# A starting stage by token halves, and one-hot rows of later pairs in an earlier step, in a kernel of clustered attention and two mixers

## The chip, the cores and the metric

The kernel runs on one core of one Trainium2 chip. The metric is device microseconds of one execution, launch included; the time before is the median of three runs.

## The reference, cut to what matters

Three layers in a row, with a float32 result; U, V and the weights arrive as 64-bit floats. The first is attention with 2 batches, 8 heads, 768 tokens and 64 numbers per head, where a query sees only the keys of its own cluster:

```python
q_assign = np.argmax(np.einsum('bhsd,hcd->bhsc', q_n, c_n), axis=-1)   # 16 clusters a head
k_assign = np.argmax(np.einsum('bhsd,hcd->bhsc', k_n, c_n), axis=-1)
mask = q_assign[:, :, :, None] == k_assign[:, :, None, :]
scores = np.where(mask, scale * np.matmul(q, k.transpose(0, 1, 3, 2)), -1000000000.0)
attn = np.exp(scores - np.max(scores, axis=-1, keepdims=True))
out = np.matmul(attn / (np.sum(attn, axis=-1, keepdims=True) + 1e-09), v)
```

Behind it stand a mixer over tokens of rank 32 (`U`, `V`) with a feed-forward part of 2048 channels, and a gated convolution mixer of 1024 channels. The change touches the attention's beginning and its helpers alone.

## The kernel before, in words

All five engines are programmed by hand: instructions of each engine run in the order in which the code emits them, and tiles carry the waits between engines. Heads go in pairs (8 pairs of 2 heads), a head in 6 tiles of 128 queries, so there are 96 steps of attention; step `n` is tile `n` in the order of heads, and `s = n % 12` is its place in its pair.

Float32 products are made of float32r matmuls of high and low parts. For one head, `ab` (128 rows) and `cd` (80 rows) are the score operands: `ab` holds parts of q and k and what is left of them after rounding, `cd` the rounded parts in rows 0 to 63 and the one-hot clusters of the query and key in rows 64 to 79, the key's scaled by 2 to the 60th, so that a pair of different clusters gets a huge negative score. For head 0 of pair 0, ScalarE and GpSimd make them from the raw tiles `rq` and `rk` (L187 to L193). For all other heads three DMAs from the POOL queue load them (`load_ops`, L104) and GpSimd subtracts (`split_ops`, L120). `load_raw` (L89) brings `rq` and `rk` of a pair on the SP queue, `load_v` (L111) the values.

Clusters of a pair: `sims` (L198) multiplies raw q and k with the normed centroids on TensorE, `sims_onehot` (L209) makes a one-hot in five VectorE operations (part 0 to 4), `onehot_t` (L228) turns it on TensorE into `oht`, `onehot_rows` (L235) copies it to `os` on ScalarE and sends its rows into `cd` with four DMAs on the SP queue. For the first pair, head 0's rows are copied directly, by ScalarE (L239) and VectorE (L240). Before the loop stand matmuls on zeros, `warm(count)` (L150), whose result nobody reads.

One `step(n)` (L577) emits, in this order: scores of tile n+2 (`s_mm`, of which `s_mm_ab` is the first half), a third of the product with the values of group g (`pv_mm`; a group is three tiles), `fin_t` of the group before (which makes `at`) or a piece of the token mixing, `sims` of the next pair when s is 2, six transposes of tile n (`t_mm`), then on ScalarE and VectorE the split of the transposed tile n-1 (`t_hi`, `t_lo`), the exponential of tile n+1 (`s_exp`), the row maximum of tile n+2 (`s_max`), the finish of a group (`fin_a` into `asb`, `fin_x`), and `prep(n)`. `fin_x` (L347) copies a finished group into `ats` on ScalarE, GpSimd then adds its halves and multiplies three tiles into `x`. `ats` has one buffer. `prep(n)` (L543) emits the work for the next pair by a table of places: one-hot parts at s = 2, 2, 3, 4, 5, raw loads and head 0's loads at 0, its split at 2, the values at 3, head 1's loads at 4, its split at 5, one-hot transposes and rows at 7.

Weights are turned from 64-bit words to float32 in jobs by `pump` (L410): in the attention loop every second step advances the one job on its way by one place of the plan `THIN` (L407): load, `job_base` on ScalarE, `job_low`, `job_high`, `job_sign` on VectorE, and put (ScalarE and GpSimd). Seven jobs belong to the loop: U, two halves of V, and four pieces of the first feed-forward chunk.

Score tiles have two PSUM buffers, so scores of tile n+2 wait for the exponential of tile n. Transposes, `at`, `oht` and similarities share three PSUM buffers (`ps_t`).

Of the kernel before, what the change touches and what calls it, by code (L numbers as in the profile page):

```python
# [24 lines left out]
P = 128  # L25
# [6 lines left out]
def tile_kernel(ctx: ExitStack, tc: tile.TileContext, qk, vv, cen, u_w, v_w, w1, w2, win, wout, conv, out):  # L32
# [55 lines left out]

    def load_raw(b, p):  # L89
        rq = a_raw.tile([P, S], F32, tag="rq", name="rq")  # L90
        rk = a_raw.tile([P, S], F32, tag="rk", name="rk")
        h0 = 2 * p
        nc.sync.dma_start(out=rq, in_=qk[b, h0:h0 + 2, :, 0, :].rearrange("h d s -> (h d) s"))
        nc.sync.dma_start(out=rk[D:2 * D], in_=qk[b, h0, :, 1, :])
        nc.sync.dma_start(out=rk[0:D], in_=qk[b, h0 + 1, :, 1, :])
        raw[b, p] = (rq, rk)

# [29 lines left out]

    cent = acon.tile([P, 2, D], F32, name="cent")
# [47 lines left out]
    nc.tensor.transpose(pc, cent.rearrange("p a d -> p (a d)"), identf)  # L176
    warm(4)
# [20 lines left out]
    def sims(b, p):  # L198
        rq, rk = raw[b, p]
        pm = ps_t.tile([P, NT * 4, NC], F32, tag="t", name="sim")  # L200
        for t in range(NT):
# [32 lines left out]

    def onehot_rows(b, p, first=False):  # L235
        pt = ohst.pop((b, p))["pt"]
        if first:
            cd = ops[b, 2 * p][1]
            nc.scalar.activation(cd[D:D + NC, 1], pt[2 * NC:3 * NC], AF.Copy, scale=BIG, bias=-BIG)  # L239
            nc.vector.tensor_copy(cd[D:D + NC, 0], pt[0:NC])  # L240
# [302 lines left out]
    def prep(n):  # L543
# [331 lines left out]
```

## Time and profile before

| | |
|---|---|
| median of three runs (lowest, highest) | 686.99 us (686.22, 689.02) |
| the profiled execution | 687.29 us |
| its span | 685.5 us |
| TensorE busy | 669.8 us (98%) |
| VectorE, ScalarE, GpSimd busy | 445.1, 373.1, 301.5 us |
| mean granted TensorE clock | 0.992 |

The span goes from the first to the last instruction; 1.8 us of the execution lie around it. A busy TensorE is not one at its peak, since matmuls overlap and their ends are modelled; how far apart the starts of equal matmuls lie says more. Times in rows are microseconds from the start of the span.

### The profile page before, as it was taken

To read this page: it belongs to the slowest core of one execution; us is meant where nothing else is said; L and a number is where in the kernel's file an instruction comes from. 1 tells how busy PE (TensorE), PEld (TensorE's weight loads), DVE (VectorE), ACT (ScalarE), POOL (GpSimd) and SP (SyncE) were. 2 spreads that over 40 slices of the span, in tenths; PEclk is the share of its full clock that TensorE was granted. 3 is DMA by queue.
4 is the path that set the end of the run, shared out by engine and by line. 5 is a ranking of instruction groups with operands and counts; after the bars stand their busy time and mean duration, and the time that the engine had idled before them with its cause. 6 is when DMAs were issued, how large, how long until landed. Compare 5 with 4: busy or idle time off the path is not lost.

```text
span 685.5 us, 10463 instructions
## 1 busy us (share of the span) xinstructions
PE 669.8 (98%) x3782; PEld 587.7 (86%) x3782; DVE 445.1 (65%) x825; ACT 373.1 (54%) x744; POOL 301.5 (44%) x391
## 2 busy tenths in 40 slices
PE   8899999999999999999999999999999999999997
PEld 6789989899999998888888888888887788888886
DVE  3888888887988898658732878775247545643400
ACT  3787869787877898425311343432133357753611
POOL 6667656676757533425530333332024644322300
PEclk8899999999999999999999999999999999999999
DMA  8986867775756611212210443342014000000111
GB/s 188 131 178 132 194 111 179 126 180 93 181 99 145 120 47 32 93 32 93 93 32 3 133 137 124 127 145 71 1 46 133 7 0 1 1 32 15 44 49 47
DMA packets 31827, 61.58 MB, mean 90 GB/s; under 512 B 15808, under 2 KB 19008, under 8 KB 31776
## 3 DMA queue, kind: packets, MB, share of 16 engines
q1 hardware_dynamic: 15632, 40.08, 19.6%
q0 software_dynamic: 16144, 20.84, 17.2%
q8 instruction: 30, 0.49, 0.3%
q14 instruction: 21, 0.17, 0.1%
HBM read 56.29 MB, written 3.15 MB: 87 GB/s over the span
## 4 chain that ended last, share of the span: by engine, by line
PE 79%; DVE 9%; issue 4%; POOL 3%; ACT 3%; DMA 2%; ACTq 0%; SPq 0%; POOLq 0%; DVEq 0%
PE g L764 10%; PE pv L328 7%; PE tr L304 6%; PE h L641 6%; PE h L642 6%; PE h L643 6%; PE a L657 5%; PE a L658 5%; PE a L659 5%; PE sc L266 4%; PE sc L277 3%; PE po L799 3%; PE po L798 3%; PE po L800 3%; PE sim L203 2%
## 5 line engine op out<-in xcount | busy, mean ns | idle before, releaser
L442 POOL TENSOR_TENSOR wl<-wx,wh 128x512 fp32r<-128x512 f32 x48 | 63.3, 1321 | 113.1 <-ACT wh L441 112.8
L317 DVE TENSOR_TENSOR pl<-tr,ph 128x384 fp32r<-128x384 f32 x192 | 97.5, 548 | 20.4 <-ACT ph L313 19.9
L313 ACT CAST ph<-tr 128x384 fp32r<-128x384 f32 x192 | 83.8, 487 | 23.5 <-PE tr L304 23.1
L283 DVE TENSOR_SCALAR_CACHE_REDUCE e<-sc 128x768 f32<-128x768 f32 x96 | 90.7, 945 | 1.9 <-PE sc L277 1.9
L646 ACT ACTIVATE rh<-h 128x512 fp32r<-128x512 f32 (+1 forms) x52 | 29.3, 563 | 112.0 <-PE h L643 112.0
L295 ACT ACTIVATE e<-sc,nb 128x768 f32<-128x768 f32 x96 | 88.1, 918 | 3.9 <-DVE e L283 3.7
L304 PE MATMUL tr<-identf,e 128*128 128x128 f32 x576 | 84.5, 278 | 4.3 <-DVE pl L317 2.5
L647 DVE SCALAR_TENSOR_TENSOR rl<-h,rh 128x512 fp32r<-128x512 f32 (+1 forms) x52 | 33.6, 647 | 83.2 <-ACT rh L646 83.2
L641 PE MATMUL h<-uh,wh 128*128 128x512 f32 (+1 forms) x208 | 78.1, 375 | 1.4 <-DVE rl L647 1.4
L657 PE MATMUL a<-rh,wh 128*128 128x512 f32 (+1 forms) x208 | 78.1, 376 | 0.5 <-DVE xa L673 0.5
L304 PEld LDWEIGHTS tr<-identf,e 128*128 128x128 f32 x576 | 66.8, 142 | 13.3 <-DVE pl L317 8.4
L658 PE MATMUL a<-rl,wh 128*128 128x512 f32 (+1 forms) x208 | 77.7, 373 | 0.3 <-DVE rl L647 0.3
L659 PE MATMUL a<-rh,wl 128*128 128x512 f32 (+1 forms) x208 | 77.6, 373 | 0.0
L643 PE MATMUL h<-uh,wl 128*128 128x512 f32 (+1 forms) x208 | 77.6, 373 | 0.0
L642 PE MATMUL h<-ul,wh 128*128 128x512 f32 (+1 forms) x208 | 77.6, 373 | 0.0
L328 PE MATMUL pv<-ph,vt 128*128 128x384 f32 x192 | 65.6, 342 | 0.2 <-ACT asb L337 0.2
L328 PE MATMUL pv<-pl,vt 128*128 128x384 f32 x192 | 64.9, 338 | 0.0
L266 PE MATMUL sc<-ab 128*128 128x384 f32 x192 | 58.6, 388 | 2.8 <-ACT e L295 2.1
L441 ACT CAST wh<-wx 128x512 fp32r<-128x512 f32 x48 | 29.8, 620 | 57.5 <-DVE wx L395 57.3
L781 POOL TENSOR_TENSOR h<-h,cv 128x768 f32<-128x768 f32 x16 | 29.6, 1851 | 64.5 <-ACT cv L780 64.5
L391 DVE SCALAR_TENSOR_TENSOR wx<-wb,wx 128x512 int32<-128x512 int32 (+3 forms) x52 | 48.8, 938 | 11.3 <-ACT wb L382 9.3
L277 PE MATMUL sc<-cd 80*128 80x384 f32 x192 | 49.8, 341 | 0.5 <-DVE cd L240 0.5
(129 smaller groups left out, 1500.0 us busy)
## 6 DMA issues: line engine op xcount, KB each, us to landing
raw<-in_w_dram SPq DMA_DIRECT2D x32, 512.0 KB, 3.8
ab<-in_qk_dram POOLq DMA_DIRECT2D x30, 384.0 KB, 5.4
cd<-in_qk_dram POOLq DMA_DIRECT2D x15, 384.0 KB, 6.6
raw<-in_win_dram SPq DMA_DIRECT2D x8, 512.0 KB, 3.6
raw<-in_wout_dram SPq DMA_DIRECT2D x8, 512.0 KB, 3.7
rq<-in_qk_dram SPq DMA_DIRECT2D x8, 384.0 KB, 4.1
rk<-in_qk_dram SPq DMA_DIRECT2D x16, 192.0 KB, 4.5
rv<-in_vv_dram SPq DMA_DIRECT2D x8, 384.0 KB, 5.7
```

The source lines that it names most:

```text
L266: nc.tensor.matmul(ps[:, f, 0:HS], ab[:, 0, c0:c0 + P], ab[:, 1, f * HS:(f + 1) * HS], start=True, stop=False)
L283: nc.vector.tensor_scalar(out=e, in0=ps[:, :, 0:HS], scalar1=-SCALE, scalar2=3e38, op0=ALU.mult, op1=ALU.min, accum_out=nb,)
L295: nc.scalar.activation(e, ps[:, :, 0:HS], AF.Exp, scale=SCALE, bias=nb, accum_out=st["sum", n // 3][:, n % 3:n % 3 + 1])
L304: nc.tensor.transpose(pt[:, k, :], e[:, i, k * P:(k + 1) * P], identf)
L317: nc.vector.tensor_sub(lo, st.pop(("t", n, i)), hi)
L328: nc.tensor.matmul(acc, vt[:, h % 2, k, :], m[:, k].rearrange("p a b -> p (a b)"), start=(k == 0 and i == 0), stop=(k == NT - 1 and i == 1),)
L641: nc.tensor.matmul(ph, wh[:, k, ws], uh[g][:, k, ts], start=(k == 0), stop=False)
L642: nc.tensor.matmul(ph, wh[:, k, ws], ul[g][:, k, ts], start=False, stop=False)
L643: nc.tensor.matmul(ph, wl[:, k, ws], uh[g][:, k, ts], start=False, stop=(k == ND - 1))
L657: nc.tensor.matmul(accs[d][:, 0:n], wh[:, i, ds_], rh, start=(f == 0), stop=False)
L658: nc.tensor.matmul(accs[d][:, 0:n], wh[:, i, ds_], rl, start=False, stop=False)
L659: nc.tensor.matmul(accs[d][:, 0:n], wl[:, i, ds_], rh, start=False, stop=(f == NH - 1))
```

## The change

The first pair's q and k are loaded and cast by halves of 384 tokens, in the order in which they are used. VectorE takes the subtraction of the key's low part (before: GpSimd). Similarities and one-hots of pair 0 are made for each half apart (`first_pair`), rows of head 0 by ScalarE alone, and `os` by VectorE. Pair 1's raw load waits for a memset behind the centroids' scaling; its similarities stand partly between the row transposes and the first scores and partly in step 0, its first two one-hot parts in step 0 too. Counts of `warm` change from 13, 4, 4, 4 to 12, 4, 5, 4, at other places. In the loop, the one-hot transposes and rows stand at s = 6 instead of 7 (for pair 1 at 5, with one-hot parts at 1, 2, 3). The first weight job starts in step 2 instead of 0, and a job takes 12 steps instead of 10, with the base two `pump` calls behind the load instead of one. Cut to the core:

```diff
-    def load_raw(b, p):
...
+    def load_raw(b, p, parts=1):
+        rq, rk = raw[b, p] if (b, p) in raw else take_raw(b, p)
         h0 = 2 * p
+        for i in range(parts):
+            c = slice(i * S // parts, (i + 1) * S // parts)
+            nc.sync.dma_start(out=rq[:, c], in_=qk[b, h0:h0 + 2, :, 0, c].rearrange("h d s -> (h d) s"))
+            nc.sync.dma_start(out=rk[D:2 * D, c], in_=qk[b, h0, :, 1, c])
+            nc.sync.dma_start(out=rk[0:D, c], in_=qk[b, h0 + 1, :, 1, c])
...
-    load_raw(0, 0)
-    load_raw(0, 1)
+    load_raw(0, 0, parts=2)
...
-    warm(13)
+    warm(12)
...
-    nc.vector.tensor_scalar(out=cent[:, 1], in0=cent[:, 0], scalar1=cn[:, 2:3], scalar2=None, op0=ALU.mult)
-    nc.vector.tensor_copy(cent[:, 0], cent[:, 1])
+    nc.vector.tensor_scalar(out=cent2, in0=cent.to_broadcast([P, 2, D]), scalar1=cn[:, 2:3], scalar2=None, op0=ALU.mult)
+
+    nc.vector.memset(take_raw(0, 1)[0][:, 0:1], 0.0)
+    load_raw(0, 1)
...
-    nc.scalar.copy(cd0[0:D, 0], rq0[0:D])
-    nc.scalar.copy(cd0[0:D, 1], rk0[D:2 * D])
-    nc.scalar.copy(ab0[D:2 * D, 0], rq0[0:D])
-    nc.scalar.copy(ab0[0:D, 1], rk0[D:2 * D])
-    nc.gpsimd.tensor_copy(ab0[D:2 * D, 1], rk0[D:2 * D])
-    nc.gpsimd.tensor_sub(ab0[D:2 * D, 1], rk0[D:2 * D], ab0[D:2 * D, 1])
-    nc.gpsimd.tensor_sub(ab0[0:D, 0], rq0[0:D], cd0[0:D, 0])
+    def split_first(half, which):
+        c = slice(half * HS, (half + 1) * HS)
+        if which == "k":
+            nc.scalar.copy(cd0[0:D, 1, c], rk0[D:2 * D, c])
+            nc.scalar.copy(ab0[0:D, 1, c], rk0[D:2 * D, c])
+            nc.gpsimd.tensor_copy(ab0[D:2 * D, 1, c], rk0[D:2 * D, c])
+            nc.vector.tensor_sub(ab0[D:2 * D, 1, c], rk0[D:2 * D, c], ab0[D:2 * D, 1, c])
+        else:
+            nc.scalar.copy(cd0[0:D, 0, c], rq0[0:D, c])
+            nc.scalar.copy(ab0[D:2 * D, 0, c], rq0[0:D, c])
+            nc.gpsimd.tensor_sub(ab0[0:D, 0, c], rq0[0:D, c], cd0[0:D, 0, c])
+
+    for half, which in ((0, "q"), (0, "k"), (1, "k")):
+        split_first(half, which)
...
+    def first_pair():
...
+        for i in range(2):
+            for part in range(5):
+                onehot_part(v, pms[i], slice(4 * NH2 * i, 4 * NH2 * (i + 1)), part)
+        warm(5)
...
+        turn(0)
+        s_mm_ab(0)
+        s_mm_ab(1)
+        warm(4)
+        turn(1)
+        rows(0, "k")
+        rows(0, "q")
+        rows(1, "k")
+        rows(0, "all")
+        rows(1, "all")
+        rows(1, "q")
+        put_rows(0, 0, os_, (1,))
...
-    THIN = {0: job_dma, 1: job_base, 2: job_low, 3: job_high, 4: job_sign, 5: job_put}
+    THIN = {0: job_dma, 2: job_base, 3: job_low, 4: job_high, 5: job_sign, 6: job_put}
...
-            if j["at"] == 5:
+            if j["at"] == max(j["plan"]):
...
-    sims(0, 0)
-    sims(0, 1)
     load_ops(0, 0, 1)
     rv0 = load_v(0, 0)
-    for part in range(5):
-        sims_onehot(0, 0, part)
-    s_mm_ab(0)
-    s_mm_ab(1)
-    warm(4)
-    onehot_t(0, 0)
-    onehot_rows(0, 0, first=True)
-    warm(4)
-    for part in range(2):
-        sims_onehot(0, 1, part)
+    first_pair()
+    split_first(1, "q")
+    sims(0, 1, range(2))
     split_ops(0, 0, 1, nc.gpsimd)
...
-            for part, at in enumerate((2, 2, 3, 4, 5)):
+            for part, at in enumerate((2, 2, 3, 4, 5) if nxt > 1 else (0, 0, 1, 2, 3)):
...
-            if s == 7:
+            if s == (6 if nxt > 1 else 5):
                 onehot_t(b, p)
                 onehot_rows(b, p)
...
-        elif n % 2 == 0:
+        elif n % 2 == 0 and n > 0:
             pump(THIN)
...
+        if n == 0:
+            sims(0, 1, range(2, NT))
...
+        if n == 0:
+            sims_onehot(0, 1, 0)
+            sims_onehot(0, 1, 1)
```

How this moves instructions is shown at three places. On the SP queue, from the first pair's values to pair 2's (`cd<-os` are one-hot rows, `u_w` and `v_w` the U and V jobs, `rq` and `rk` the raw tiles), it stood so before:

```order
L114 DMA rv<-in_vv_dram 128x768
L247 DMA cd<-os 16x768 x2
L376 DMA raw<-in_u_w_dram 128x384
L114 DMA rv<-in_vv_dram 128x768
L247 DMA cd<-os 16x768 x4
L376 DMA raw<-in_v_w_dram 32x768 x3
L93 DMA rq<-in_qk_dram 128x768
L94 DMA rk<-in_qk_dram 64x768
L95 DMA rk<-in_qk_dram 64x768
```

and now:

```order
L118 DMA rv<-in_vv_dram 128x768
L265 DMA cd<-os 16x768 x2
L452 DMA raw<-in_u_w_dram 128x384
L118 DMA rv<-in_vv_dram 128x768
L265 DMA cd<-os 16x768 x4
L94 DMA rq<-in_qk_dram 128x768
L95 DMA rk<-in_qk_dram 64x768
L96 DMA rk<-in_qk_dram 64x768
L452 DMA raw<-in_v_w_dram 32x768 x3
```

Pair 2's raw tiles changed places with the first half of V; the four rows of pair 1 above them belong to step 5 instead of 7.

On POOL, from the first pair's splits to the split of pair 1's second head (`ab<-rq,cd` and `ab<-rk` are pair 0's first head; `ab<-in_qk_dram` and `cd<-in_qk_dram` load a head's operands), it stood so before:

```order
L191 CAST ab<-rk 64x768
L192 TENSOR_TENSOR ab<-rk,ab 64x768
L193 TENSOR_TENSOR ab<-rq,cd 64x768
L107 DMA ab<-in_qk_dram 64x1536
L108 DMA ab<-in_qk_dram 64x1536
L109 DMA cd<-in_qk_dram 64x1536
L116 DMA vt<-in_vv_dram 128x6x64 x2
L125 TENSOR_TENSOR ab<-rq,ab 64x768
L125 TENSOR_TENSOR ab<-rk,ab 64x768
L465 TENSOR_TENSOR vt<-rv,vt 128x12x64
```

and now:

```order
L203 TENSOR_TENSOR ab<-rq,cd 64x384
L198 CAST ab<-rk 64x384 x2
L111 DMA ab<-in_qk_dram 64x1536
L112 DMA ab<-in_qk_dram 64x1536
L113 DMA cd<-in_qk_dram 64x1536
L120 DMA vt<-in_vv_dram 128x6x64 x2
L203 TENSOR_TENSOR ab<-rq,cd 64x384
L129 TENSOR_TENSOR ab<-rq,ab 64x768
L129 TENSOR_TENSOR ab<-rk,ab 64x768
L532 TENSOR_TENSOR vt<-rv,vt 128x12x64
```

The loads of pair 0's second head went ahead of one half subtraction, the one key subtraction left POOL, and the second half of q stands between those loads and their splits. What follows on POOL keeps its order.

On ScalarE, around the copy `os` of the one-hot rows of pair 2 (in pair 1; `asb` and `ats` finish a group, `wb` is a weight job's base, `tt` and `mt` belong to the token mixing), it stood so before:

```order
L337 COPY asb<-pv 128x384
L313 CAST ph<-tr 128x3x128 x2
L295 ACTIVATE e,sum<-sc,nb 128x768
L350 COPY ats<-at 128x384
L242 ACTIVATE os<-oht,ohs 64x768
L313 CAST ph<-tr 128x3x128 x2
L295 ACTIVATE e,sum<-sc,nb 128x768
L503 CAST tt_284<-mt 96x128
```

and now:

```order
L413 COPY asb<-pv 128x384
L257 ACTIVATE os<-oht,ohs 64x768
L458 ACTIVATE wb<-raw 96x384
L389 CAST ph<-tr 128x3x128 x2
L371 ACTIVATE e,sum<-sc,nb 128x768
L426 COPY ats<-at 128x384
L389 CAST ph<-tr 128x3x128 x2
L371 ACTIVATE e,sum<-sc,nb 128x768
L570 CAST tt_293<-mt 96x128
```

`os` moved from behind `ats` to before it, one exponential ahead, and a base now stands directly behind it.

## Rows read from the trace of the kernel before

**Rows 1.** The chain that ended last, share of the span by engine, from the page
```profile
PE 79%; DVE 9%; issue 4%; POOL 3%; ACT 3%; DMA 2%; ACTq 0%; SPq 0%; POOLq 0%; DVEq 0%
```

**Rows 2.** The chain of the first 60 us in order: start, length, what
```profile
22.59 7.04 DMA ab<-in_qk_dram
...
35.91 5.90 DMA ab<-in_qk_dram
...
46.79 0.80 POOL x L358 x3
...
47.61 0.06 ACT ats L350
...
49.80 0.62 PE sc L266 x2
...
55.94 2.61 PE sim L203 x24
```

**Rows 3.** ScalarE's timeline, second `ats` copy: start, length, line, operation [idle before]
```profile
47.61 0.48 ACT L350 COPY ats<-at 128x384 f32<-128x384 f32 x1 [0.71 <-POOL x L358]
```

**Rows 4.** The timeline of the starting stage, all engines
```profile
5.25 0.83 ACT L187 CAST cd<-rq 64x768 fp32r<-64x768 f32 x1 [0.43 <-DMA rq<-in_qk_dram]
...
8.68 1.80 POOL L193 TENSOR_TENSOR ab<-rq,cd 64x768 fp32r<-64x768 f32 x1
...
9.55 0.56 DVE L215 TENSOR_REDUCE mx<-sim 128x24 f32<-128x384 f32 x1 [3.12 <-PE sim L203]
...
20.08 0.95 DVE L283 TENSOR_SCALAR_CACHE_REDUCE e<-sc 128x768 f32<-128x768 f32 x1
...
22.12 1.00 PE L266 MATMUL sc<-ab 128*128 128x384 f32 x2 [2.11 <-ACT e L295]
```

**Rows 5.** POOL's timeline: splits, loads of pair 1's second head, a later split
```profile
16.64 1.80 POOL L125 TENSOR_TENSOR ab<-rq,ab 64x768 fp32r<-64x768 f32 x1 [2.70 <-DMA ab<-in_qk_dram]
...
31.49 1.83 POOL L125 TENSOR_TENSOR ab<-rk,ab 64x768 fp32r<-64x768 f32 x1 [1.88 <-issue]
...
35.35 0.57 POOL L107 DMA_DIRECT2D ab<-in_qk_dram  x1
...
41.95 1.84 POOL L125 TENSOR_TENSOR ab<-rq,ab 64x768 fp32r<-64x768 f32 x1 [4.97 <-DMA ab<-in_qk_dram]
...
91.64 1.82 POOL L125 TENSOR_TENSOR ab<-rk,ab 64x768 fp32r<-64x768 f32 x1
```

**Rows 6.** The SP queue's timeline: the U job and pair 1's one-hot rows
```profile
22.02 0.58 SPq L376 DMA_DIRECT2D raw<-in_u_w_dram  x1
...
40.83 2.68 SPq L247 DMA_DIRECT2D cd<-os  x4
```

**Rows 7.** Windows: stretch, length, busy us of PE, PEld, DVE, ACT, POOL, clock, DMA
```profile
20.00:22.10 2.10, 0.01 (x1) 0.00 (x0) 1.92 (x5) 1.10 (x4) 2.10 (x3) 1.00 0.14 31
22.10:25.50 3.40, 3.38 (x13) 3.29 (x14) 1.52 (x3) 1.75 (x5) 1.57 (x3) 0.51 0.75 181
```

**Rows 8.** TensorE's timeline: starts of the scores in steps 8, 9 and 93
```profile
39.70 0.62 PE L266 MATMUL sc<-ab 128*128 128x384 f32 x2
...
42.48 0.61 PE L266 MATMUL sc<-ab 128*128 128x384 f32 x2
...
266.56 0.60 PE L266 MATMUL sc<-ab 128*128 128x384 f32 x2
```

**Rows 9.** ScalarE's timeline: the first `os` in the loop, a base, the next cast
```profile
39.81 0.99 ACT L242 ACTIVATE os<-oht,ohs 64x768 fp32r<-64x768 bf16 x1 [0.77 <-PE oht L232]
...
133.36 0.67 ACT L382 ACTIVATE wb<-raw 128x512 f32<-128x512 f32 x1
133.92 0.47 ACT L313 CAST ph<-tr 128x384 fp32r<-128x384 f32 x1
```

**Rows 10.** VectorE's timeline: two operations that took far longer than their like
```profile
91.76 2.12 DVE L391 SCALAR_TENSOR_TENSOR wx<-wb,wx 96x384 int32<-96x384 int32 x1
...
131.73 2.15 DVE L226 TENSOR_TENSOR oh<-eq,m 128x384 bf16<-128x384 bf16 x1
```

More of the change, by code (lines that the diff above doesn't have):

```diff
@@ L87, in tile_kernel, with take_raw @@
     vts = {}
-    def load_raw(b, p):
-        rq = a_raw.tile([P, S], F32, tag="rq", name="rq")
-        rk = a_raw.tile([P, S], F32, tag="rk", name="rk")
+    def load_raw(b, p, parts=1):
+        rq, rk = raw[b, p] if (b, p) in raw else take_raw(b, p)
         h0 = 2 * p
[L93 to L96, printed above, removed]
+        for i in range(parts):
[3 more added lines that the diff above has]
+            nc.sync.dma_start(out=rk[0:D, c], in_=qk[b, h0 + 1, :, 1, c])
+    def take_raw(b, p):
+        raw[b, p] = tuple(a_raw.tile([P, S], F32, tag=t, name=t) for t in ("rq", "rk"))
+        return raw[b, p]
     def take_ops(b, p, j):
@@ L186, in tile_kernel, with sims @@
     ab0, cd0 = take_ops(0, 0, 0)
-    nc.scalar.copy(cd0[0:D, 0], rq0[0:D])
-    nc.scalar.copy(cd0[0:D, 1], rk0[D:2 * D])
-    nc.scalar.copy(ab0[D:2 * D, 0], rq0[0:D])
-    nc.scalar.copy(ab0[0:D, 1], rk0[D:2 * D])
-    nc.gpsimd.tensor_copy(ab0[D:2 * D, 1], rk0[D:2 * D])
-    nc.gpsimd.tensor_sub(ab0[D:2 * D, 1], rk0[D:2 * D], ab0[D:2 * D, 1])
-    nc.gpsimd.tensor_sub(ab0[0:D, 0], rq0[0:D], cd0[0:D, 0])
+    def split_first(half, which):
[11 more added lines that the diff above has]
+        split_first(half, which)
     ohst = {}
-    def sims(b, p):
+    def sims(b, p, tiles=range(NT)):
         rq, rk = raw[b, p]
-        pm = ps_t.tile([P, NT * 4, NC], F32, tag="t", name="sim")
-        for t in range(NT):
+        if (b, p) not in ohst:
+            ohst[b, p] = {"pm": ps_t.tile([P, NT * 4, NC], F32, tag="t", name="sim")}
+        pm = ohst[b, p]["pm"]
+        for t in tiles:
             for i, (r, cb) in enumerate(((rq, cbq), (rk, cbk))):
@@ L206, in sims @@
                 )
-        ohst[b, p] = {"pm": pm}
     def sims_onehot(b, p, part):
-        sh = [P, NT * 4, NC]
         v = ohst[b, p]
@@ L214, in sims_onehot, with onehot_part @@
             v["mx"] = a_oh.tile([P, NT * 4, 1], F32, tag="mx", name="mx")
-            nc.vector.tensor_reduce(out=v["mx"], in_=v["pm"], axis=AX.X, op=ALU.max)
+            v["eq"] = a_oh.tile([P, NT * 4, NC], BF16, tag="eq", name="eq")
+            v["m2"] = a_oh.tile([P, NT * 4, 1], BF16, tag="m2", name="m2")
+            v["oh"] = a_oh.tile([P, NT * 4, NC], BF16, tag="oh", name="oh")
+        onehot_part(v, v["pm"], slice(0, NT * 4), part)
+    def onehot_part(v, pm, gs, part):
+        sh = [P, gs.stop - gs.start, NC]
+        mx, eq, m2, oh = (v[k][:, gs] for k in ("mx", "eq", "m2", "oh"))
+        if part == 0:
+            nc.vector.tensor_reduce(out=mx, in_=pm, axis=AX.X, op=ALU.max)
         elif part == 1:
-            v["eq"] = a_oh.tile(sh, BF16, tag="eq", name="eq")
-            nc.vector.tensor_tensor(out=v["eq"], in0=v["pm"], in1=v["mx"].to_broadcast(sh), op=ALU.is_ge)
+            nc.vector.tensor_tensor(out=eq, in0=pm, in1=mx.to_broadcast(sh), op=ALU.is_ge)
         elif part == 2:
-            nc.vector.tensor_tensor(out=v["eq"], in0=v["eq"], in1=iota, op=ALU.mult)
+            nc.vector.tensor_tensor(out=eq, in0=eq, in1=iota[:, gs], op=ALU.mult)
         elif part == 3:
-            v["m2"] = a_oh.tile([P, NT * 4, 1], BF16, tag="m2", name="m2")
-            nc.vector.tensor_reduce(out=v["m2"], in_=v["eq"], axis=AX.X, op=ALU.max)
-        else:
-            v["oh"] = a_oh.tile(sh, BF16, tag="oh", name="oh")
-            nc.vector.tensor_tensor(out=v["oh"], in0=v["eq"], in1=v["m2"].to_broadcast(sh), op=ALU.is_equal)
+            nc.vector.tensor_reduce(out=m2, in_=eq, axis=AX.X, op=ALU.max)
+        else:
+            nc.vector.tensor_tensor(out=oh, in0=eq, in1=m2.to_broadcast(sh), op=ALU.is_equal)
     def onehot_t(b, p):
@@ L233, in onehot_t, with onehot_rows, put_rows @@
         ohst[b, p]["pt"] = pt
-    def onehot_rows(b, p, first=False):
+    def onehot_rows(b, p):
         pt = ohst.pop((b, p))["pt"]
[L237 to L240, printed above, removed]
         os_ = a_oh.tile([4 * NC, S], F32R, tag="os", name="os")
         nc.scalar.activation(os_, pt, AF.Identity, scale=ohs[:, 0:1], bias=ohs[:, 1:2])
-        for j in range(1 if first else 0, 2):
+        put_rows(b, p, os_, range(2))
+    def put_rows(b, p, os_, heads):
+        for j in heads:
             cd = ops[b, 2 * p + j][1]
@@ L247, in onehot_rows, with turn, rows @@
                 nc.sync.dma_start(out=cd[D:D + NC, i].bitcast(F32), in_=os_[r0:r0 + NC].bitcast(F32))
+    def first_pair():
+        NH2 = NT // 2
+        rq, rk = raw[0, 0]
+        cd = ops[0, 0][1]
+        v = {
+            "mx": a_oh.tile([P, NT * 4, 1], F32, tag="mx", name="mx"),
+            "eq": a_oh.tile([P, NT * 4, NC], BF16, tag="eq", name="eq"),
+            "m2": a_oh.tile([P, NT * 4, 1], BF16, tag="m2", name="m2"),
+            "oh": a_oh.tile([P, NT * 4, NC], BF16, tag="oh", name="oh"),
+        }
+        os_ = a_oh.tile([4 * NC, S], F32R, tag="os", name="os")
+        pms, pts = [], []
+        for i in range(2):
+            pm = ps_t.tile([P, NH2 * 4, NC], F32, tag="t", name="sim")
+            for k, (r, cb) in enumerate(((rq, cbq), (rk, cbk))):
+                for t in range(NH2):
+                    c0 = (i * NH2 + t) * P
+                    nc.tensor.matmul(
+                        pm[:, 4 * t + 2 * k:4 * t + 2 * k + 2, :].rearrange("p g c -> p (g c)"),
+                        r[:, c0:c0 + P], cb[:, 0], start=True, stop=True,
+                    )
+            pms.append(pm)
+        for i in range(2):
+            for part in range(5):
+                onehot_part(v, pms[i], slice(4 * NH2 * i, 4 * NH2 * (i + 1)), part)
+        warm(5)
+        def turn(i):
+            pt = ps_t.tile([4 * NC, HS], BF16, tag="t", name="oht")
+            for t in range(NH2):
+                g0 = 4 * (i * NH2 + t)
+                nc.tensor.transpose(pt[:, t * P:(t + 1) * P], v["oh"][:, g0:g0 + 4].rearrange("p g c -> p (g c)"), identb)
+            pts.append(pt)
+        def rows(i, what):
+            cs = slice(i * HS, (i + 1) * HS)
+            if what == "k":
+                nc.scalar.activation(cd[D:D + NC, 1, cs], pts[i][2 * NC:3 * NC], AF.Copy, scale=BIG, bias=-BIG)
+            elif what == "q":
+                nc.scalar.copy(cd[D:D + NC, 0, cs], pts[i][0:NC])
+            else:
+                nc.vector.tensor_scalar(
+                    out=os_[:, cs], in0=pts[i], scalar1=ohs[:, 0:1], scalar2=ohs[:, 1:2], op0=ALU.mult, op1=ALU.add)
+        turn(0)
[10 more added lines that the diff above has]
+        put_rows(0, 0, os_, (1,))
     NQ = B * H * NT
```

5 lines of the change are left out of this document (3 added, 2 removed).

## The prediction

> **What bounds the kernel now.** I read the chain of waits first, then that chain in order of time over the first 60 us, then the timelines of GpSimd (POOL), of the DMA queue (SP) and of the starting stage, then the starts of the score matmuls. Over the whole span the chain lies on TensorE for 79% [rows 1]: from the attention loop on, other engines count only where they hold TensorE up. The exception is the beginning. There the chain runs through POOL: the load of pair 1's first head (22.59 to 29.63), that of its second head (35.91 to 41.81), three multiplications into x that end at 47.6, ScalarE's copy into `ats` at 47.61, and only then TensorE's scores of step 12 at 49.80 [rows 2]. The reason is in the order. `ats` has one buffer, so the copy of the second group (step 10) waits until POOL has read the first; POOL works in order, and those reads stand behind the splits of both heads of pair 1, each behind its transfer. TensorE's own path ends at nearly the same time, for the copy had stood for only 0.71 us [rows 3]. So a sooner first score brings well under a microsecond by itself; what counts is how far POOL's chain moves.
>
> **1. The starting stage, TensorE's side.** The first cast starts at 5.25, having waited 0.43 us for its transfer, the first one-hot operation at 9.55, the first row maximum at 20.08, step 0 at 22.12 [rows 4]. Half a cast is worth about 0.45 of the 0.83 us, half a POOL subtraction about 1.0 of 1.80 [rows 4]. A pair's similarities take 2.61 us [rows 2]: pair 0's, in two halves, end near 8.5, and pair 1's no longer stand ahead of the transposes. VectorE has two key subtractions (0.5 each) and ten half operations of some 0.36 (from 0.56 for 384 columns [rows 4]) with gaps: first one-hots at 10.2, second at 12.1. Transposes, copies of rows on ScalarE (0.45 each) and the score matmuls follow: first row maximum near 14.0, step 0 near 16.1. That is 6.0 us sooner on TensorE. It assumes that the dummies hold its clock; if not, it is 1.5 less.
>
> **2. POOL's chain.** It is gated in a new place. The second half of q is cast on ScalarE behind the four copies of rows, near 14.6, and POOL's subtraction of it stands ahead of the splits of pair 0's second head. So these start at 15.7, against 16.64 [rows 5]: -0.95. Ends: -1.9 if the transposes don't wait for dummies, +0.7 if the clock falls.
>
> **3. Pair 1, first head.** Its second half was split at 31.49, 8.9 us after its issue at 22.59; beside it ran 576 KB on the SP queue (the U job of 192 KB, issued at 22.02 [rows 6], and the values, 384 KB; sizes are the shapes in the order above times 4 bytes). The second head, with next to nothing beside it, was split at 41.95, 6.0 us after its issue at 35.91 [rows 2, 5]. So 576 KB cost 2.9 us, 5 us per MB. The change sends the U job behind the first pair's rows, some 5 us ahead: -1.0 (ends 0 and -1.9, the whole wait between 29.63 and 31.49).
>
> **4. Pair 1, second head.** Here the change gives back. SP waits for the one-hot rows of pair 1 until 40.83 [rows 6], and pair 2's raw q and k stand behind them. In the changed order the rows go out in step 5 (near 28.7) and nothing holds the 768 KB behind them, nor the 288 KB of V: they are issued near 31 to 34, and the second head at about 33.3 (35.35 [rows 5] less 2). No row shows this meeting. If it were all over in time it would cost 0, if all of it lay ahead 5.3. A third of it, 350 KB, is my estimate, since the raw tiles have a start of 2 us: +1.75. The Trainium skill (DMA: Bandwidth & Descriptors, section Issuing engines are not separate DMA queues) says that transfers of all issuing engines run on the same 16 DMA engines and interleave. The two heads above agree with it; read to its end it gives the 5.3, which is rival B.
>
> Sum of 2 to 4: -0.95 - 1.0 + 1.75 = -0.2 us for the release of `ats`. The other -6 us of TensorE turn into a wait.
>
> **5. The clock after that wait.** Steps 0 to 11 took 27.7 us (22.12 to 49.80), some 25.5 without the low clock and the stall, so TensorE would want step 12 near 41.6; with `ats` released 0.2 sooner it gets it near 49.6, and stands for over 5 us around steps 10 and 11. After 2.1 us without work (20.0 to 22.1) the next 3.4 us ran at a granted 0.51, nearly all at 1.2 GHz [rows 7]; that cost 1.7 us. I take +1.5 (ends 0 and 1.7).
>
> **6. The steps of the later pairs.** From step 12 (49.80) to step 93 (266.56) are 81 steps [rows 2, 8]. A plain step takes 2.07 us, and what comes on top in some, by the starts of the same rows, is 27 x 0.33 for `at`, 6 x 2.63 for similarities, 6 x 0.66 for one-hot transposes, 7 x 1.33 for `mt`, 6 x 0.33 and 4 x 0.43 for later mixing: 209.3 of 216.8 us. The rest, 7.4 us, is waiting. Two pieces, 1.53 and 1.42, come from VectorE operations of some 0.6 us that took 2.12 and 2.15 (91.76 and 131.73) [rows 10], the first while POOL ran a split (91.64) [rows 5]. So an operation on one of the two can hold up the other's for its whole length. The Trainium skill (SBUF — State Buffer, section Who interferes with whom) gives as the condition a VectorE instruction with two SBUF inputs against a GpSimd one that reads SBUF, which speaks against the new key subtractions beside POOL's casts (rival D). Some 3 us are weight operations that meet one-hot parts in steps 3 to 6 of a pair, and 1.5 lie in step 7.
> The longer job plan puts every weight job in the same places: base in step 6, shift and or in 8 and 10, sign in 0, put in 2. That clears VectorE; I leave 1.2 us of the 5.9 outside step 7. But the rows' copy `os` and the base now stand together on ScalarE at the end of step 6. In pair 0, where nothing covered it, `os` (39.81) stretched a step to 2.78 us (39.70 to 42.48, 0.71 over plain) [rows 8, 9]; from pair 1 on `mt` in step 8 (1.33) hid it. Moved a step ahead it loses that cover: 2.78 plus the base (0.56, from 133.36 to the next start at 133.92 [rows 9]) against 2.07 + 0.33 is 0.94, in six pairs 5.6. So 6.8 in place of 7.4: -0.6. Ends: -6.2 if the burst is absorbed, +2 if VectorE's collisions stay as well. Pair 0's own burst and the similarities moved into step 0 lie under the wait of part 4. The rows' sooner sending is worth nothing to TensorE later: its waits list no row of `cd` beyond the first.
>
> **Sum.** 687.29 - 0.2 + 1.5 - 0.6 = 688.0 for a run like the profiled one. That run is 0.3 over the median of the three, so I forecast 687.7: no change that can be told (0.5%, 3.4 us, is about what can). Its own range is 684.5 to 690.4: -2.0 to +2.5 for POOL's chain, 0 to 1.7 for the clock, -2 to +1 for the pairs, not all at one end.
>
> **Rivals.**
> *A, POOL does not gate.* If the release of `ats` came 6 us sooner too, the whole of part 1 would stay and no clock would be lost: 687.0 - 6.0 - 0.6 = 680.4. For it: POOL stands idle for the transfers of both heads, so only they would have to be sooner. Against: the splits and transfers in its line are as many and as long as before. Chance 0.08.
> *B, slower.* Pair 2's raw tiles and V hold up the second head's transfer for the whole 5.3 us: 687.0 - 1.95 + 5.3 + 1.7 - 0.6 = 691.4. It decides from about 4 us of delay on. For: the first head waited that way. Against: the start of 2 us. Chance 0.17.
> *C, the burst is absorbed.* If ScalarE has caught up by step 7, part 6 is worth -6.2: 687.0 - 0.2 + 1.5 - 6.2 = 682.1. For: in step 7 TensorE has 0.33 more to do than in pair 0's case. Against: pair 0's 0.71, without a base. Chance 0.15.
> *D, the halves don't land sooner* (or VectorE's key subtractions are locked out by POOL's casts, 0.5 us each): step 0 comes only 4 us sooner and POOL at +0.7: 687.0 + 0.7 - 1.0 + 1.75 + 1.2 - 0.6 = 689.1. Chance 0.1, inside no change.
>
> **How the numbers follow.** The forecast has 0.5, of which 0.02 at its lower edge count as faster; A 0.08 and C 0.15 are faster too, D 0.1 is no change, B 0.17 slower. So faster 0.25, same 0.58, slower 0.17. The range reaches down to C and up nearly to B, 682.0 to 691.0; A and half of B lie outside.
>
> **What would show it.** Step 0 near 16; POOL's first split of pair 0's second head near 15.7; raw q of pair 2 issued near 31 and the split of pair 1's second head not before 41; ScalarE's second `ats` copy directly after POOL's x, near 47; TensorE empty for some 5 us before it and the clock near 0.5 behind; later pairs losing about 0.9 us in step 7 and little elsewhere. If `ats` is released near 42, or step 7 takes 2.4 us, I am wrong on the side of too slow.

## The result, and the profile after

The changed kernel takes 694.37 us (median of nine, 692.17 to 695.73), the kernel before 689.58 (nine, 686.22 to 692.11): ratio 1.0069, 95% interval 1.0046 to 1.0092. It is slower by 0.7%, where 687.7 us and no change were forecast, and it lies above the range. The profiled execution before (687.29) is one of its shorter ones, so the two profiles differ by more than the medians: spans of 685.5 and 692.2, 6.7 us. Those 6.7 are what is taken apart here.

The shares of the chain that ended last, from the page, against [rows 1]:

```profile
PE 78%; DVE 8%; issue 3%; DMA 3%; ACT 3%; POOL 2%; ACTq 0%; POOLq 0%; DVEq 0%
```

The shares say little; the chain of the first 60 us in order of time (start, length, what), against [rows 2], says it:

```profile
21.93 8.28 DMA ab<-in_qk_dram x2
...
34.91 10.04 DMA ab<-in_qk_dram
...
46.97 1.80 POOL ab L129
...
48.85 0.22 POOL sum L681
...
49.83 0.80 POOL x L434 x3
...
50.64 0.03 ACT ats L426
...
53.05 0.79 PE sc L342 x2
```

It is the same chain as before, through POOL to ScalarE's copy into `ats`, but the load of pair 1's second head takes 10.04 us in place of 5.90. What ran beside it stands on the SP queue:

```profile
29.53 2.41 SPq L265 DMA_DIRECT2D cd<-os  x4
31.99 0.57 SPq L94 DMA_DIRECT2D rq<-in_qk_dram  x1
32.61 0.50 SPq L95 DMA_DIRECT2D rk<-in_qk_dram  x1
33.16 0.59 SPq L96 DMA_DIRECT2D rk<-in_qk_dram  x1
33.79 1.51 SPq L452 DMA_DIRECT2D raw<-in_v_w_dram  x3
```

Pair 2's raw tiles and V go out between 32 and 35, as forecast (31 to 34). Pair 1's values, which stand ahead of the second head on POOL's own queue (two loads of 192 KB), were slower too: they landed 5.4 and 8.0 us after their issue, before 3.1 and 3.5. ScalarE and VectorE both stand until POOL is through; their timelines, with the idle time and its releaser in brackets:

```profile
50.64 0.48 ACT L426 COPY ats<-at 128x384 f32<-128x384 f32 x1 [11.10 <-POOL x L434]
```
```profile
49.10 0.18 DVE L429 RECIPROCAL rs<-sum 128x3 f32<-128x3 f32 x1 [8.90 <-POOL sum L681]
```

TensorE's windows (stretch, length, busy us of PE, PEld, DVE, ACT, POOL, then clock and DMA) show the beginning at full clock in this execution, and the price of the wait:

```profile
0.00:20.00 20.00, 17.60 (x111) 13.45 (x112) 14.52 (x43) 12.84 (x26) 12.86 (x39) 1.00 1.19 194
```
```profile
40.50:51.50 11.00, 1.61 (x10) 1.29 (x9) 0.85 (x2) 0.86 (x3) 6.09 (x8) 0.74 0.54 92
51.50:53.40 1.90, 1.83 (x8) 1.25 (x7) 1.86 (x5) 1.90 (x6) 1.71 (x3) 0.50 0.00 0
53.40:56.30 2.90, 2.90 (x13) 2.81 (x12) 2.20 (x7) 1.57 (x5) 2.60 (x7) 0.56 0.67 210
```

After 9.4 us with next to nothing to do, TensorE ran at half clock, the lower level of 1.2 GHz, for most of 4.8 us.

The starts of the score matmuls place the 6.7 us. Steps 0, 11, 12, 14 and 93 of the changed kernel, then steps 11 and 14 of the kernel before (the others in [rows 4, 2, 8]):

```profile
16.25 0.61 PE L342 MATMUL sc<-ab 128*128 128x384 f32 x2 [0.35 <-ACT e L371]
...
40.12 0.60 PE L342 MATMUL sc<-ab 128*128 128x384 f32 x2
...
52.83 1.01 PE L342 MATMUL sc<-ab 128*128 128x384 f32 x2
...
58.72 0.59 PE L342 MATMUL sc<-ab 128*128 128x384 f32 x2
...
272.36 0.60 PE L342 MATMUL sc<-ab 128*128 128x384 f32 x2
```
```profile
47.23 0.60 PE L266 MATMUL sc<-ab 128*128 128x384 f32 x2
...
54.28 0.59 PE L266 MATMUL sc<-ab 128*128 128x384 f32 x2
```

Step 0 stands at 16.25 (before 22.12), step 11 at 40.12 (47.23), step 12 at 52.83 (49.80): 7.1 ahead became 3.0 behind. Step 14 is 4.4 behind, so the clock took 1.4. Step 93 stands at 272.36 (266.56), 5.8 behind: the later pairs took 1.4. The last 0.9 lie in the mixers, in pieces of a few tenths.

### The profile page after: what moved, and what is told of

Its sections match the earlier page's. It is cut to its first block, busy times and chain, and to the rows that moved or that the text cites. A ratio compares the mean times of both kernels' runs of the same rounds, so it can differ in the third digit from the quotient of the medians.

```text
span 692.2 us, 10474 instructions
## 1 busy us (share of the span) xinstructions
PE 666.3 (96%) x3782; PEld 586.0 (85%) x3782; DVE 445.8 (64%) x833; ACT 373.0 (54%) x750; POOL 298.9 (43%) x392
## 4 chain that ended last, share of the span: by engine, by line
PE 78%; DVE 8%; issue 3%; DMA 3%; ACT 3%; POOL 2%; ACTq 0%; POOLq 0%; DVEq 0%
PE g L836 10%; PE tr L380 7%; PE pv L404 7%; PE h L713 5%; PE h L715 5%; PE h L714 5%; PE a L730 5%; PE a L729 5%; PE a L731 5%; PE sc L342 3%; PE sc L353 3%; PE po L870 3%; PE po L871 3%; PE po L872 3%; DMA ab<-in_qk_dram 3%
```

## The experiments

Times are medians; a ratio is to the kernel before in the same session, with its 95% interval. The changed kernel's is 1.0069. It was timed in another session than the runs below, so a difference to it is uncertain by some 1.2 us: that far apart are medians and ratios in places. What a step "loses" is its length beyond a plain step and what that step has on top by design (0.33 us for `at`, 0.66 for one-hot transposes, and so on).

### Does pair 2's raw load hold up the second head?

```diff
     def prep(n):
         pair, s = divmod(n, 2 * NT)
+        if n == 9:
+            nc.vector.memset(take_raw(0, 2)[0][:, 0:1], 0.0)
```

> The changed kernel with one memset more on VectorE in step 9, into the raw query tile of pair 2, so that SP cannot issue pair 2's raw tiles (and V behind them) before about 38.5 us; in the changed kernel they went out from 31.99 to 35.3. Theory 1 (these 1.06 MB share the DMA engines with the load of pair 1's second head, issued 34.34 to 35.98): the load lands some 6 us after 34.9 as in the kernel before (5.90) and not 10.0 us after, POOL's first split of it starts near 41.1 in place of 45.09, ScalarE's second ats copy near 46.6 in place of 50.64, and the run is 4.0 us shorter (690.3 where the changed kernel takes 694.4). Rival (the load is long for a reason of its own, such as its place on the POOL queue): the split still starts near 45 and the time stays at 694.

Measured: 690.95 us, ratio 1.0013 (0.9999 to 1.0027), 3.4 below the changed kernel. Raw q went out at 40.02. In the DMA view of 32 to 50 us (x, KB each, median us to landing), the changed kernel and this one have:

```profile
ab<-in_qk_dram POOLq DMA_DIRECT2D x2, 384.0 KB, 9.5
```
```profile
ab<-in_qk_dram POOLq DMA_DIRECT2D x2, 384.0 KB, 5.6
```

and this run's POOL splits the second head at 41.96 in place of 45.09, ScalarE copies at 47.55 in place of 50.64:

```profile
41.96 1.84 POOL L129 TENSOR_TENSOR ab<-rq,ab 64x768 fp32r<-64x768 f32 x1 [5.26 <-DMA ab<-in_qk_dram]
```
```profile
47.55 0.48 ACT L426 COPY ats<-at 128x384 f32<-128x384 f32 x1 [6.08 <-POOL x L434]
```

Both are 0.9 later than expected, of which 0.7 is a later issue (35.08). Theory 1 holds: the transfer is as long as what lies beside it makes it. TensorE's wait shrank from 10.6 to 5.6 us but did not go: TensorE is still through with step 11 sooner than POOL's chain. Of these 5.0 us only 3.1 come from POOL (step 12 at 49.73 in place of 52.83); the other 1.9 are a later step 11 (42.05 in place of 40.12), for the granted clock of this execution was 0.72 from 16 to 22 us.

### Is it the one buffer of `ats`?

Two kernels. The first has `bufs=3` for `ats`; the second has this line too:

```diff
-            nc.gpsimd.tensor_scalar(out=sm, in0=sm, scalar1=1e-9, ...
+            nc.vector.tensor_scalar(out=sm, in0=sm, scalar1=1e-9, ...
```

> The changed kernel with three buffers for ats instead of one, nothing else. Theory 1 (the one ats buffer is what holds TensorE between steps 11 and 12, as the prediction said): the wait of 10.6 us goes, and with it the 1.4 us at the lower clock behind it; 12 us less, near 682.4. Rival (a second wait lies right under it: VectorE's reciprocal of the sums, L429, waits until 49.10 for POOL's addition to the sums, L681, which stands behind the same splits, and the split of the transposed tile stands behind it on VectorE): ScalarE's copy goes sooner, VectorE still stands from 40.2 to about 49, TensorE comes back some 1.5 us sooner, and the time is near 692.9.

> Three buffers for ats, and the small addition to the sums (128x3) on VectorE instead of POOL, so that neither ScalarE nor VectorE waits for POOL's order in step 10. Both theories of the run with three buffers alone expect the wait of 10.6 us and the low clock behind it gone: score of step 12 near 42.5 in place of 52.83, near 682.4, less some 0.1 us of VectorE for each of 32 groups where VectorE has no slack. If yet another wait on POOL's order stands behind (the values' low part, L633, which ended at 52.4), TensorE stops a few steps later and the gain is smaller, 4 to 8 us.

Buffers alone: 693.44 us, ratio 1.0038 (1.0025 to 1.0051), 0.9 below the changed kernel by the medians and 2.1 by the ratios; step 12 came 1.15 sooner. The rival holds. ScalarE's copy goes at once, and VectorE stands until 49.76 all the same:

```profile
41.67 0.48 ACT L426 COPY ats<-at 128x384 f32<-128x384 f32 x1 [0.20 <-PE at L420]
```
```profile
49.76 0.18 DVE L429 RECIPROCAL rs<-sum 128x3 f32<-128x3 f32 x1 [7.63 <-POOL sum L681]
```

With the addition off POOL as well: 687.74 us, ratio 0.9962 (0.9949 to 0.9975). The wait and the low clock are gone:

```profile
43.00 0.59 PE L342 MATMUL sc<-ab 128*128 128x384 f32 x2
```

Step 14 comes 11.3 us sooner than in the changed kernel, near the 12 expected. By step 93 only 6.4 are left: 4.9 were lost again in pairs 1 to 4. The two largest losses, 1.35 and 1.00 in one step, stand where VectorE ran a job's sign for 2.23 us and the moved addition, 128x3, for 1.25, each while POOL ran a split.

> The kernel before with three buffers for ats and, in steps 4 to 15, the small addition to the sums on VectorE, so that TensorE is bound by nothing of POOL's there; in the changed kernel the same two edits took 6.7 us off. Theory 1 (in the kernel before TensorE's own path ended at nearly the same time as POOL's: ScalarE's second ats copy had stood for 0.71 us): 0.5 to 1 us less at most, inside what a comparison tells, 689.5 to 690.4. Rival (POOL held the kernel before by more than that, by waits that the profile of one execution hid): 2 us less or more.

Measured on the kernel before, with the same edits in steps 4 to 15: 690.96 us, ratio 1.0014 (0.9996 to 1.0033). Theory 1 holds by the time: without the sooner beginning, freeing `ats` gives nothing. In its profiled execution other waits stood in steps 3 and 4 (1.40 and 1.14 us), one of them ScalarE's base for the U job's transfer (1.41 us). So it does not show how close the two paths lay.

### What do the rows in step 6 cost?

Two kernels, one edit each (the second puts the base into step 4):

```diff
-            if s == (6 if nxt > 1 else 5):
+            if s == (7 if nxt > 1 else 5):
```
```diff
-    THIN = {0: job_dma, 2: job_base, ...
+    THIN = {0: job_dma, 1: job_base, ...
```

> The changed kernel with the one-hot transposes and rows of the later pairs (2 to 7) back in step 7 of a pair; the new job plan stays. Theory 1 (the copy os and the base wb stand together on ScalarE at the end of step 6, and the next step has no cover for them): step 7 loses 0 to 0.5 us in place of 0.92 to 1.03, in six pairs 3 to 5.5 us, so 689 to 691 from 694.4. Rival (what is lost in step 7 belongs to the job plan, or comes back in step 8, where the token mixing follows): less than 1.5 us, near 693.5.

> The changed kernel with the base of a weight job one pump call sooner, in step 4 of a pair in place of step 6; os stays in step 6. Both theories of the run with the rows back in step 7 put the 0.92 to 1.03 us of step 7 on what stands on ScalarE at the end of step 6. Theory 1 (os and base share it by their lengths there, 0.99 and 0.54 to 0.67): without the base step 7 loses 0.3 to 0.5 us, in six pairs 3 us less, near 691.4, unless the base costs the same in step 4. Rival (os alone is enough to uncover TensorE, the base only lengthens what it hides): step 7 keeps 0.7 or more (pair 0's os alone cost 0.71 in the kernel before), time 693 or more.

Rows back in step 7: 690.31 us, ratio 0.9995 (0.9981 to 1.0010), 4.1 below the changed kernel. Step 7 loses 0.02 to 0.16 us instead of 0.92 to 1.03, and nothing comes back in step 8. Base in step 4: 692.66 us, ratio 1.0047 (1.0024 to 1.0069); step 7 loses 0.47 in each of the six pairs, and step 5 now 0.25 to 0.37 in each. ScalarE in the changed kernel, and with the base away:

```profile
72.73 0.99 ACT L257 ACTIVATE os<-oht,ohs 64x768 fp32r<-64x768 bf16 x1 [0.57 <-PE oht L251]
73.63 0.54 ACT L458 ACTIVATE wb<-raw 96x384 f32<-96x384 f32 x1
74.07 0.83 ACT L389 CAST ph<-tr 128x384 fp32r<-128x384 f32 x2
```
```profile
72.42 0.99 ACT L257 ACTIVATE os<-oht,ohs 64x768 fp32r<-64x768 bf16 x1 [0.57 <-PE oht L251]
73.31 0.83 ACT L389 CAST ph<-tr 128x384 fp32r<-128x384 f32 x2
```

`os` and base each cost about their half of the 0.92 to 1.03: the cast of the next step stands behind both. Theory 1 holds in both runs, and the time of the second follows it only in part, because the base costs nearly as much in its new place.

From step 14 to step 93 the kernel before took 212.3 us (54.28 to 266.56), the changed one 213.6 (58.72 to 272.36), this one with the rows in step 7 208.6 (58.61 to 267.25). So the rest of the change, of which the new job plan stands in these steps, gave 3.6 us, and the rows in step 6 took 5.0.

### Together, and what then comes next

Three `ats` buffers, rows in step 7, and the addition on VectorE in steps 4 to 15 only:

```diff
-            nc.gpsimd.tensor_scalar(out=sm, ...
+            (nc.vector if n < 16 else nc.gpsimd).tensor_scalar(out=sm, ...
```

> The changed kernel with three edits together: three ats buffers, the addition to the sums on VectorE in steps 4 to 15 only (on POOL after them), rows of the later pairs back in step 7. By the runs of each alone: the wait of 10.6 us and the 1.4 us of low clock go (12), and 4.1 us of step 7. In the run with the addition on VectorE everywhere 4.9 us of the 12 were lost again in pairs 1 to 4; Theory 1 (those were VectorE additions of 128x3 that took 1.25 and 1.42 us while POOL ran a subtraction, and two meetings of a like kind): most of it is not lost here, 678 to 680. Rival (POOL, which is now late against TensorE, meets VectorE's one-hot operations in pairs 1 to 3 whatever carries the addition): 681 to 683.5.

Measured: 683.23 us, ratio 0.9900 (0.9873 to 0.9928), faster than both kernels by 1% and more. The time lies in the rival's range, for steps 5, 13, 16 and 23 lost 1.37, 0.93, 0.82 and 0.79. The last three are of the rival's kind, other VectorE work that met a POOL subtraction: a weight job's sign that took 1.61 us at 47.62, an or that took 1.94 at 75.74, and a one-hot part, whose like in the changed kernel takes 0.35:

```profile
57.67 1.54 DVE L241 TENSOR_TENSOR eq<-eq,iota 128x384 bf16<-128x384 bf16 x1
```

Step 5 is the moved addition; POOL and VectorE:

```profile
28.00 1.81 POOL L129 TENSOR_TENSOR ab<-rq,ab 64x768 fp32r<-64x768 f32 x1 [4.82 <-DVE pl L393]
28.09 0.08 DVE L359 DVE_READ_ACCUMULATOR e<-sc 128x1 f32 x1
28.09 1.75 DVE L681 TENSOR_SCALAR sum<-sum 128x3 f32<-128x3 f32 x1
```

The addition ends as POOL's split ends. Alone, in the run on the kernel before, it took a tenth of that:

```profile
35.84 0.17 DVE L609 TENSOR_SCALAR sum<-sum 128x3 f32<-128x3 f32 x1
```

The sign of a job in another step, on top of the three edits:

```diff
-    ... 2: job_base, 3: job_low, 4: job_high, 5: job_sign, 6: job_put}
+    ... 2: job_base, 3: job_low_high, 4: job_sign, 6: job_put}
```

> The kernel of the three edits with one more: the job plan's shift and or together in step 8 (where the token mixing gives TensorE 1.33 us more) and the sign in step 10 in place of step 0. In the changed kernel steps 1 of pairs 5, 6 and 7 lost 0.87, 0.86 and 0.53 us, where VectorE ran the sign (0.68) behind the mixing's addition (0.68), and some other steps of pairs 4 to 7 0.2 to 0.5. Theory 1 (the sign in step 0 is what tips step 1): these 2.3 us go, 2 us less than the kernel of the three edits. Rival (the mixing's additions alone are enough, or the sign costs as much in step 10): within 0.7 us of it.

Measured: 687.79 us, ratio 0.9978 (0.9953 to 1.0002), 4.6 above. Of the theory one half holds: steps 1 of pairs 5 to 7 lose nothing now. But step 9 takes 0.4 to 1.0 us longer than without the edit in pairs 2 to 6, and shift and or met both of POOL's splits in pair 1, where steps 21 and 22 lost 5.3 (part of it at a low clock behind the wait):

```profile
69.60 1.85 POOL L129 TENSOR_TENSOR ab<-rq,ab 64x768 fp32r<-64x768 f32 x1 [4.31 <-DMA ab<-in_qk_dram]
...
70.00 1.66 DVE L463 TENSOR_SCALAR wx<-raw 96x384 int32<-96x384 int32 x1
...
71.52 1.80 POOL L129 TENSOR_TENSOR ab<-rk,ab 64x768 fp32r<-64x768 f32 x1
...
71.69 2.04 DVE L467 SCALAR_TENSOR_TENSOR wx<-wb,wx 96x384 int32<-96x384 int32 x1
```

The addition on ScalarE for n < 16, without and with the hold on pair 2's raw tiles (the memset of the first experiment):

```diff
-            nc.gpsimd.tensor_scalar(out=sm, ...
+            if n < 16:
+                nc.scalar.activation(sm, sm, AF.Copy, bias=1e-9)
+            else:
+                nc.gpsimd.tensor_scalar(out=sm, ...
```

> The kernel of the three edits, with the addition to the sums of steps 4 to 15 on ScalarE instead of VectorE (a copy with a bias, 128x3). In the kernel of the three edits that addition took 1.75 us on VectorE at 28.09, from just after the start of POOL's first split of pair 1 (28.00) to its end, and step 5 lost 1.37 us; steps 13, 16 and 23 lost 0.93, 0.82 and 0.79. Theory 1 (VectorE's reading and writing of SBUF is shut out while POOL subtracts; ScalarE's is not): the addition takes some 0.2 us on ScalarE wherever it falls, step 5 loses 0.3 or less, 1 to 1.5 us less than the 683.2 of the three edits: near 682. Rival (VectorE is shut out by the next operation instead, or ScalarE's place costs as much): within 0.5 us of 683.2.

> The kernel with the addition on ScalarE, and with pair 2's raw tiles and V held until step 9 as in the run that held them alone. There the hold was worth 3.4 to 4 us because TensorE waited for POOL. Theory 1 (with three ats buffers and the addition off POOL nothing waits for pair 1's second head any more, so the same hold, with its transfer just as much shorter, is worth next to nothing on TensorE): within 1 us of the same kernel without the hold. Rival (an earlier POOL also meets VectorE less in steps 13 to 23, where the kernel of the three edits lost 2.5 us): 1.5 to 2.5 us less, near 680.

Measured: 686.56 us, ratio 0.9951 (0.9929 to 0.9973), and 683.46 us, ratio 0.9914 (0.9889 to 0.9940). On ScalarE the addition takes 0.19 to 0.22 us wherever it falls, and step 5 loses nothing, so the mechanism holds; the time does not follow (682 was expected). Its executions lie between 682.68 and 691.78 (those of the three edits between 682.36 and 692.79), and the profiled one is the fastest, so what holds up the others was not seen. The hold was worth 3.1 us here by the medians, which is the rival's side, but the intervals overlap and the two profiled executions (682.68 and 683.08) do not show it. In the profile with the hold a new wait shows, of TensorE for one-hot rows:

```profile
72.90 0.72 PE L353 MATMUL sc<-cd 80*128 80x384 f32 x2 [2.50 <-DMA cd<-os]
```

Step 22 lost 4.3 us to it. Two last kernels start from there: all later raw tiles held too (the edit shown), and rows in step 6 again (the line of the third group, undone).

```diff
-        if n == 9:
-            nc.vector.memset(take_raw(0, 2)[0][:, 0:1], 0.0)
+        if s == (9 if pair == 0 else 10) and pair + 2 < B * NP:
+            nc.vector.memset(take_raw(*divmod(pair + 2, NP))[0][:, 0:1], 0.0)
```

> The kernel with three ats buffers, the addition to the sums on ScalarE in steps 4 to 15, rows in step 7 and pair 2's raw tiles held until step 9, with the raw tiles of every later pair held too, until step 10 of the pair two before (a memset on VectorE each). In the run that held pair 2's alone, the first score of pair 2 waited until 72.76 for its one-hot rows, which had been issued at 65.45, with pair 3's raw tiles and the second half of V (issued from 67.95 on) right behind: 4.3 us in step 22. Theory 1 (the raw tiles share the DMA engines with the rows, as they did with the second head): with the raw tiles issued behind, the rows land in 3 us or so, step 22 loses nothing, and the executions lie closer together: near 680, highest and lowest within 3 us. Rival (the rows were late for a reason of their own, and the raw tiles now come late for the similarities): 683.5 or more.

> The kernel with three ats buffers, the addition on ScalarE and pair 2's raw tiles held until step 9, with the one-hot rows of the later pairs in step 6 as in the changed kernel. Theory 1 (step 6 costs 0.92 to 1.03 us in six pairs whatever else is done; against that the rows go out a step sooner, which spares pair 2's wait of 4.3 us where it occurs): 683.5 - 4.3 + 5.9 = 685, and 687 to 688 against an execution without that wait. Rival (with TensorE no longer waiting, the sooner rows are worth more than they cost, as the change meant): below 683.

All raw tiles held: 688.97 us, ratio 1.0003 (0.9979 to 1.0027). Theory 1 fell: the rows took as long, with pair 3's raw tiles not issued before 75.92. What ran beside them was POOL's load of pair 2's second head, from 65.38 on; that this made them late was not tried. The 4.5 us that this run loses after step 14 against the kernel it starts from lie in pairs 3 to 5 and were not taken apart. From the chain of that run, then POOL:

```profile
67.07 6.90 DMA cd<-os
```
```profile
65.38 0.60 POOL L111 DMA_DIRECT2D ab<-in_qk_dram  x1
```

Rows in step 6: 687.09 us, ratio 0.9966 (0.9951 to 0.9980); step 7 loses 0.91 to 1.04 in each of six pairs, pair 2's rows are in time. By the medians the sooner rows cost more than they bring, as theory 1 had it, but the profiles do not show that: from step 14 to step 93 both profiled executions took 213.5 us, some 5.2 lost to the rows against 4.3 won in step 22 and less waiting elsewhere. The 4.1 us by which the profiled execution with rows in step 6 is behind lie before step 14, where the two kernels emit the same order: there a one-hot part on VectorE took 2.43 us in place of 1.58 beside POOL's work in step 2, and the granted clock from 22 to 30 us was 0.66 in place of 1.00. So a start that is alike in code can come out 4 us apart. 683.2 and 683.5 us, not to be told apart, are the best that these runs gave.

## Why the prediction was wrong, step by step

*What bounds the kernel now.* Right in the main: POOL's chain, not TensorE's, set step 12, and the 5.9 us gained at step 0 turned into a wait. Wrong in one point: `ats` with one buffer was called the reason. VectorE's reciprocal waits for POOL's sum 1.5 us earlier in the same chain (49.10 against 50.64), and freeing `ats` alone brought step 12 only 1.15 us sooner.

*Part 1.* Right: first row maximum at 13.87 (14.0), step 0 at 16.25 (16.1), clock held. That it held is partly luck: of the eleven profiles of kernels with the same beginning, eight show a granted clock of 0.50 or 0.72 from 16 to 22 us.

*Parts 2 and 3.* Pair 0's second head was split from 16.03 on (15.7, before 16.64), but the next load went out at 21.93, only 0.1 sooner, not 0.95: POOL waited 0.3 for the load ahead of the splits, and the values' low part started 0.3 sooner and ran longer. The first head's second split came at 30.48, 1.0 sooner, as part 3 had it. So the second head was issued 1.0 sooner, at 34.34, and not 1.95.

*Part 4 is the step that failed.* "A third of it, 350 KB, is my estimate, since the raw tiles have a start of 2 us: +1.75." The load took 4.1 us longer (10.04 against 5.90 [rows 2]), over three quarters of the whole 5.3, and the gate on SP's transfers took it back. The raw tiles were nowhere near through after 2 us: they had been issued from 31.99 to 33.75 and took 3.6 to 5.2 us to land. A third was chosen between bounds of 0 and 5.3 without a row, where the one comparison at hand, the first head against the second [rows 2, 5], had charged a load with all the bytes beside it. The Trainium skill (DMA: Bandwidth & Descriptors, section Issuing engines are not separate DMA queues), which the prediction named there, says that transfers of all issuing engines interleave on the same DMA engines. The trace agrees with it; a share it does not give. With part 2 the load put the release of `ats` at +3.0 instead of -0.2. That is rival B, which had 0.17: "decides from about 4 us of delay on", and that is where it came; its time, 691.4, lacks what the later pairs and the mixers added.

*Part 5.* Right: 1.4 for 1.5.

*Part 6.* The burst of `os` and base was right in place, cause and size: 0.92 to 1.03 in six pairs, 5.9 in all for 5.6. The two long VectorE operations of [rows 10] did go. What was mis-sized is "I leave 1.2 us of the 5.9 outside step 7": by the prediction's own count steps 12 to 93 hold 8.8 us of waiting (219.5 less 209.3 and the clock's 1.4), and without step 7's 5.9 that leaves 2.9. Of these 2.3 stand in steps 1 of pairs 5, 6 and 7, where VectorE runs the token mixing's addition and then the sign, which the new plan puts into step 0:

```profile
184.71 0.68 DVE L582 TENSOR_TENSOR x<-x,mu 128x512 f32<-128x512 f32 x1
...
185.31 0.68 DVE L471 SCALAR_TENSOR_TENSOR wx<-wb,wx 128x512 int32<-128x512 int32 x1
...
185.91 1.01 DVE L393 TENSOR_TENSOR pl<-tr,ph 128x384 fp32r<-128x384 f32 x2
```

I had looked for what left VectorE's crowded steps, not for what stands in the steps the work went to. So the pairs cost 1.4 more than before instead of 0.6 less. "The rows' sooner sending is worth nothing to TensorE" holds for these two kernels, not for the ones in which TensorE no longer waits for POOL.

*The sum.* Against the profiled execution 0.7 was forecast and 6.7 came: 3.2 more from parts 2 and 4 (some 0.9 and 2.4), 2.0 from part 6, 0.9 in the mixers, which no part had; what makes these was not looked into. *Rivals A, C and D* did not occur: POOL did gate, the burst was not absorbed, the halves landed in time, and VectorE's two key subtractions took 0.55 and 0.83 us where 0.5 each was counted.

## What to carry to other kernels

Where a stage is bound by a chain of transfers on another engine, a sooner start of the bound engine turns into a wait (here 5.9 us into 10.6, and 1.4 of clock) until every wait on that chain is cut: two of them stood 1.5 us apart, and cutting the visible one alone gave 1 to 2 us of 12. When an order change lets loads go out sooner, ask whose transfer they now run beside, and charge that one with all of their bytes unless a row shows otherwise. When work moves to another step to clear an engine, count what already stands there, in the last repetitions of the loop too.

## What the runs showed of the hardware

- Transfers of SP's queue (1.06 MB) that were issued from 3 us ahead of a POOL load until its start stretched it from 5.90 to 10.04 us, and holding them back gave 6.3 (35.64 to the split at 41.96). Small rows met the like: 48 KB a row, 2.3 us to land in the kernel before, took 6.9 beside POOL's load of a head, and there it was SP's transfer, issued 1.1 us behind POOL's, that was late. Why what was issued first went almost wholly first was not tried.
- A VectorE operation of 0.17 us (128x3) took 1.75 beside a POOL subtraction, ending with it; on ScalarE the same took 0.19 to 0.22. The Trainium skill (SBUF — State Buffer, section Who interferes with whom) names this form, tensor_scalar, among those that can take the port pair shared with GpSimd, whoever issues first for the whole instruction. The trace agrees, and shows that an operation's own size does not bound its price: the other engine's instruction does.
